# Other assumed delays and other offsets in a build-time scheduler, for two layers of segmented attention and SwiGLU

## Chip, cores and metric

One core of a Trainium2 chip runs the kernel. The metric is device time in microseconds (us) of one execution; the median of three runs before the change is 1984.57 us (1983.71 to 1984.62). In views and code the engines are called PE (TensorE, matmuls), PEld (its weight load, which overlaps the matmuls), DVE (VectorE), ACT (ScalarE), POOL (GpSimd) and SP (SyncE, which here only issues DMA transfers).

## What is computed

Two layers, each an attention part and a feed-forward part, on 2048 rows of 512 numbers, with 32 heads of 16 columns. Attention goes over four segments of 512 rows: a causal softmax inside the segment, plus a read from a running memory matrix that earlier segments filled.

```python
def _A_ref(x, wq, wk, wv, wo, beta):          # H = 32, Dh = 16, N = 4 segments of L = 512
    ...
    for s in range(N):
        qs, ks, vs = q[:, :, s], k[:, :, s], v[:, :, s]
        logits = jnp.einsum("bhqd,bhkd->bhqk", qs, ks) * scale + mask
        p = _softmax(logits, axis=-1)
        a_dot = jnp.einsum("bhqk,bhkd->bhqd", p, vs)
        pq = phi(qs)
        num = jnp.einsum("bhld,bhde->bhle", pq, M)
        den = jnp.einsum("bhld,bhd->bhl", pq, z)[..., None] + 1e-6
        outs.append(g * num / den + (1.0 - g) * a_dot)
        pk = phi(ks)
        M = M + jnp.einsum("bhld,bhle->bhde", pk, vs)
        z = z + jnp.einsum("bhld->bhd", pk)
    ...
    return o @ wo
def _B_ref(x, w_gate, w_up, w_down):          # 512 -> 1792 -> 512
    return (_silu(x @ w_gate) * (x @ w_up)) @ w_down
x = x + _A_ref(_layernorm(x), ...); x = x + _B_ref(_layernorm(x), ...)   # twice
```

## The kernel before

The program is not written in the order in which it runs. `Program.op` (L93) records 13,456 operations, each with its engine, a cost in us, a priority, and the operations that it depends on: those that wrote what it reads, that read what it overwrites, or that used its buffer before. Then `Program.issue` (L144) plays the program through once, with one clock for each engine. On the engine that can start earliest it takes, among the operations that are ready by then, the one with the lowest priority number, and emits its instruction. The result is one fixed row of instructions for each engine; on the chip every engine goes through its row in order and waits on semaphores. Two tables steer the plan. `LAT` (L38) is the delay that the planner believes lies between the end of an operation on one engine and the start of one that needs it on another. The offsets in `OFF`, `PRE` and `EP` (L30 to L32) set the priorities: in `at(v)` a number in units of one attention step (`TA`) or one feed-forward step (`TF`), from which an operation's place is worked out. Priorities do not make an operation wait; they only choose among those that are ready.

```python
            t[e] = start + o.cost
...
            end = t[e] + o.post
...
            for s in o.succ:
                s.ready = max(s.ready, end + LAT[e].get(s.eng, 0.0))
```

The work itself, in float32 that is split into a high and a low part (three matmuls in place of one, `mm3`, L281):

- **Attention** goes in 32 units a layer (4 segments, 4 head groups, 2 halves; `U`, L398). `qk_proj` (L454) projects q and k for a group (12 matmuls, L278), ScalarE copies the bank to `raw` (L464), GpSimd splits it (L465, L467), and two transfers write it to scratch memory (`scrq`, `scrk`; L479, L480), from which `load3` (L486) reads it back in another layout into `cq` and `ck` (L504, L509). `phiq` and `phik` are finished on VectorE (L474).
- `mx_units` (L514) makes the row maxima. A **score fill** (L527) writes 256, 384 or 512 columns of scores to one of two PSUM banks `pmx`, and VectorE reduces each (L534, 128 to 512 columns). The next fill of the same bank, two fills later, has to wait for those reductions. There are 768 fills in the program. The maxima are transposed (L543) and sent by a small DMA into the spare row of `cq`.
- `at_units` (L553) makes the scores again (L574, into three banks `plt`), ScalarE exponentiates them (L580), GpSimd masks the diagonal blocks (L588), and a value matmul in column groups (L603, bank `ppv`) follows.
- `mem_read` (L650) and `mem_update` (L666, L678) serve the memory; `wo_proj` projects the output; `ln_pre` and `ln_fin` make the layer norm (L349 to L361 on VectorE and GpSimd), transpose it on TensorE (L369) and copy it on ScalarE (L373) and VectorE (L374).
- **Feed-forward** (`ffn`, L800): seven chunks of 256 columns by four blocks of 512 rows; gate and up projections (L857), SiLU (L866), product (L867, L870), down projection (L884) and sum (L889). Its first steps are planned into the last attention units.

Projection matmuls (L278), and near the end of a layer those of the feed-forward part, need nothing from the engines that work on the scores. They are what the planner can put between two score matmuls: this text calls them filler. The banks `pj` are a pool of two that the planner gives out itself.

Of the kernel before, what the change touches and what calls it, by code (L numbers as in the profile page):

```python
# [26 lines left out]
WOT = ("pmx_0", "pmx_1", "pj", "pj")  # L27
EARLY_AT = (23, 25, 26)
TA, TF = 15.5, 16.7
OFF = {'qe': (0.481, 1.468), 'at': (0.2, 1.0), 'mx': (-0.666, 0.16), 'lf': (-0.709, -0.318), 'mr': (0.865, 0.781), 'mu': (0.556, 0.139), 'wo': (0.263, 1.746), 'qk': (-0.342, 0.41), 'v': (-0.3, 0.518), 'lp': (0.034, 1.108)}  # L30
PRE = {'c': -1.851, 'mb': 0.212, 'lv': -1.7, 'lo': -0.87, 'gate': -1.0, 'v': -1.534, 'dv': 0.12, 'qk1': -1.2, 'mx': -1.0}
EP = {'w': -1.935, 'wn': 0.178, 'ln': -3.0, 'dn': -0.06, 'up': -2.73}  # L32
POOL_W = ""
TABLE = 1.28
DRAIN = {("full", "cols"): 0.195, ("cols", "full"): 0.095}


LAT = dict(  # L38
    pe=dict(pe=0.01, act=0.2, dve=0.2, sp=0.19),
    act=dict(act=0.22, dve=0.13, pe=0.27, pool=0.2, sp=0.15),  # L40
    dve=dict(dve=0.13, act=0.13, pe=0.25, pool=0.16, sp=0.12),
    pool=dict(pool=0.1, dve=0.06, pe=0.13, act=0.1, sp=0.05),
    sp=dict(act=1.2, dve=1.2, pe=1.2, pool=1.2, sp=1.2),
)


# [195 lines left out]
def infini_swiglu(ctx: ExitStack, tc: tile.TileContext, x, wq, wk, wv, wo, beta, wg, wu, wd, out,  # L242
# [78 lines left out]
    def make_gate():  # L321
        for i in range(4):
            dma(lambda i=i: nc.sync.dma_start(bet.ap[32 * i:32 * i + 32],
                                              bass.AP(tensor=beta.tensor, offset=beta.offset + 2 * i,
                                                      ap=[[0, 32], [8, NG], [1, 2]])), [], [(bet, i)], kb=20)
        act(8, lambda: nc.scalar.activation(gnot.ap, bet.ap, AF.Exp), [bet], [gnot])
        dve(8, lambda: nc.vector.tensor_scalar_add(gnot.ap, gnot.ap, 1.0), [gnot], [gnot])
        dve(64, lambda: nc.vector.reciprocal(gnot.ap, gnot.ap), [gnot], [gnot])
        dma(lambda: nc.sync.dma_start(ginv.ap, bass.AP(tensor=beta.tensor, offset=beta.offset, ap=[[0, 128], [1, H]])),
            [], [ginv], kb=20)  # L330
        act(H, lambda: nc.scalar.activation(ginv.ap, ginv.ap, AF.Exp, scale=-1.0), [ginv], [ginv])
        dve(H, lambda: nc.vector.tensor_scalar_add(ginv.ap, ginv.ap, 1.0), [ginv], [ginv])
# [59 lines left out]
    def attention(lay, x_in, x_out, slots, T, hook):  # L392
# [7 lines left out]
        def at(v):  # L400
            P.prio = base + v * T

        def load_w(nm, w, tags):
            wh, wl = sb(S8[nm + "h"], T8, F32R), sb(S8[nm + "l"], T8, F32R)
            W[nm] = (wh, wl)
            for kc in range(KC):
                raw = sb(tags, [128, 512])
                dma(lambda kc=kc, raw=raw: nc.sync.dma_start(raw.ap, w[kc * 128:(kc + 1) * 128, :]), [], [raw])
                split(raw, lambda t: t, wh, wl, lambda t, kc=kc: t[:, kc, :], kc, 512)

        def load_w4(nm, w, slot):
            wh, wl = sb(S8[nm + "h"], T8, F32R), sb(S8[nm + "l"], T8, F32R)
            W[nm] = (wh, wl)
            raw = sb(S8[slot], T8)
            for kc in range(KC):
                dma(lambda kc=kc: nc.sync.dma_start(raw.ap[:, kc, :], w[kc * 128:(kc + 1) * 128, :]), [], [(raw, kc)])
                act(512, lambda kc=kc: nc.scalar.copy(wh.ap[:, kc, :], raw.ap[:, kc, :]), [(raw, kc)], [(wh, kc)],
                    sbuf=True)
                if nm in POOL_W:
                    gp(1.23, lambda kc=kc: nc.gpsimd.tensor_sub(wl.ap[:, kc, :], raw.ap[:, kc, :],  # L420
                                                                wh.ap[:, kc, :].bitcast(F32)),
                       [(raw, kc), (wh, kc)], [(wl, kc)])
                else:
                    dve(512, lambda kc=kc: nc.vector.tensor_sub(wl.ap[:, kc, :], raw.ap[:, kc, :],
                                                                wh.ap[:, kc, :].bitcast(F32)),
                        [(raw, kc), (wh, kc)], [(wl, kc)])
# [6 lines left out]
        def ln_fin(s, t, tag="pj"):  # L433
            if t == 0:
                xT[s] = (sb(S8["xh"], TX, F32R), sb(S8["xl"], TX, F32R))
            ln_transpose(XN.pop((s, t)), xT[s][0], xT[s][1], t, tag)
# [49 lines left out]
        def load3(u):  # L486
            s, n, h = U[u]
            g = GRP[s, n]
            if u < NB:
                cq = sb(S8[f"c{u}"], [128, 4, 512], F32R)  # L490
                ck = CK.get(u) or sb(f"ck{u}", [128, 2, 512], F32R)
                C3[u] = cq, ck
                pr, P.prio = P.prio, base + PRE["c"] * T
                after = [XTL] if u else []
# [147 lines left out]
        def mem_read(s, n):  # L642
            g = GRP[s, n]
            phi, m = g["phiq"], Mb[n]
            g["mem"] = mem = sb("mem", [128, 4, 128], ring=2)
            for t0 in (0, 2):
                ps, r = bank("pj"), sb("rm", [128, 2, 8, 1], ring=2)
                pv = lambda ps=ps: ps.ap[:, 0:16 * VW].rearrange("p (t h e) -> p t h e", t=2, e=VW)
                for t in range(2):
                    pe(8 * VW, 4, lambda t=t, t0=t0, ps=ps: nc.tensor.matmul(  # L650
                        ps.ap[:, 8 * VW * t:8 * VW * (t + 1)], lhsT=phi.ap[:, (t0 + t) * 128:(t0 + t + 1) * 128],
                        rhs=m.ap.rearrange("p h e -> p (h e)"), start=True, stop=True), [m, phi], [(ps, t)])
                gv = lambda: ginv.ap[:, 8 * n:8 * n + 8].rearrange("p (t h e) -> p t h e", t=1, e=1).to_broadcast([128, 2, 8, 1])
                dve(16, lambda pv=pv, r=r, gv=gv: nc.vector.scalar_tensor_tensor(
                    out=r.ap, in0=pv()[:, :, :, DH:VW], scalar=1e-6, in1=gv(), op0=OP.add, op1=OP.mult),
                    [ps, ginv], [r])
                dve(110, lambda r=r: nc.vector.reciprocal(r.ap, r.ap), [r], [r])
                dve(256, lambda pv=pv, r=r, t0=t0: nc.vector.tensor_mul(
                    mem.ap[:, t0:t0 + 2].rearrange("p t (h e) -> p t h e", e=DH), pv()[:, :, :, 0:DH],
                    r.ap.to_broadcast([128, 2, 8, DH])), [ps, r], [(mem, t0)])  # L660
# [47 lines left out]
        if lay == 0:  # L708
# [6 lines left out]
            load_w4("k", wk, "p1")  # L715
            at(PRE["lv"])
            load_w4("v", wv, "th")
            at(PRE["lo"])
            load_w4("o", wo, "tl")
# [3 lines left out]
        else:  # L723
# [5 lines left out]
            load_w("k", wk, RAW)  # L729
            at(PRE["lv"])  # L730
            load_w("v", wv, RAW)
        XTL = xT[0][0]
        at(PRE["mb"])
        for n in range(NG):
# [7 lines left out]
        if lay == 0:  # L742
            at(PRE["gate"])
            make_gate()
# [8 lines left out]
        for i, f in enumerate(mxu):  # L753
            at(PRE["mx"] + (OFF["mx"][1] - OFF["mx"][0]) * i / len(mxu))
            f()
        for u, (s, n, h) in enumerate(U):
# [3 lines left out]
            def put(units, lo, hi, rank):  # L760
                for i, f in enumerate(units):
                    items.append((u + i / max(1, len(units)) , rank, i, u + lo + (hi - lo) * (i + 0.5) / len(units), f))

            g2 = u // 2 + 2
            put(at_units(u), *OFF["at"], 0)
            if u + 1 < NU:
                put(mx_units(u + 1), *OFF["mx"], 1)
            if w8 == 4 and s + 1 < nseg:
                put([lambda t=t: ln_fin(s + 1, t) for t in range(4)], *OFF["lf"], 2)
            if h == 1 and u + 1 < NU and U[u + 1][0] > 0:  # L770
                put([lambda: mem_read(*U[u + 1][:2])], *OFF["mr"], 3)
# [28 lines left out]
    def ffn(base, x_in, x_out, slots, T):  # L800
        X, XT, Wc = {}, {}, {}

        def hold(b):
            XT[b] = (sb(slots[f"H{b}"], TX, F32R), sb(slots[f"L{b}"], TX, F32R))

        def at(v):
            P.prio = base + v * T
# [94 lines left out]
        for c in range(NF):  # L902
            for b in range(4):
                v = 4 * c + b
                if c == 0:
                    if 0 < b <= E:
                        yield
                    at(v + EP["ln"])
                    hold(b)
# [15 lines left out]
                up_at = v + (EP["up"] if v < E else 0.0)
                at(up_at)
# [68 lines left out]
```

## Time and profile before

| | us |
|---|---|
| median of three runs | 1984.57 |
| the profiled execution, first to last instruction (span) | 1980.6 |
| TensorE busy | 1929.6 |
| VectorE busy | 1139.6 |
| ScalarE busy | 759.6 |
| GpSimd busy | 473.3 |

The profile covers one execution; the 4.0 us between its span and the median are the launch and the end around it. A busy TensorE is not one at its peak: matmuls overlap, and the view sets the end of one 0.39 us after its start for 512 columns, while the next may start after 0.23 us. So an idle time of TensorE in these views begins only when the modelled end of the last matmul is past.

### The profile page before, as it was taken

How to read it: one execution, taken by the hardware profiler on the slowest of the kernel's cores; microseconds unless marked ns; L12 is line 12 of the kernel's file. 1: busy time of each engine (PE TensorE's matmuls, PEld its weight loads, DVE VectorE, ACT ScalarE, POOL GpSimd, SP SyncE). 2: the span in 40 equal slices, each digit the busy share in tenths (PEclk: the TensorE clock that was granted, in tenths of full speed). 3: DMA queues.
4: the chain of work that ended last, by engine and by line, in shares of the span. 5: the costliest groups of instructions: out<-in, count | busy, mean ns of one | idle time of the engine just before them, and what ended most of it. 6: DMA issues, size and time to landing. Idle time of an engine off the chain costs nothing. (4 is left out here: it accounts for less than half of the span.)

```text
span 1980.6 us, 31412 instructions
## 1 busy us (share of the span) xinstructions
PE 1929.6 (97%) x11136; PEld 1491.9 (75%) x11136; DVE 1139.6 (58%) x3446; ACT 759.6 (38%) x1758; POOL 473.3 (24%) x731
## 2 busy tenths in 40 slices
PE   7999999999999999999999999999999999999999
PEld 5677676776678888888876777677767788888887
DVE  6877767688644333333557677786784433333333
ACT  4655564545522212121335655555554212211211
POOL 5333443434410000000233444353343100000000
PEclk9999999999999999999999999999999999999999
DMA  7434434446131100010364353353652301100002
GB/s 245 120 111 129 129 102 146 134 155 194 54 117 33 32 22 22 22 33 22 101 192 124 105 158 123 109 151 113 181 161 70 96 11 32 32 22 11 17 1 85
DMA packets 101548, 184.00 MB, mean 93 GB/s; under 512 B 12816, under 2 KB 28176, under 8 KB 101392
## 3 DMA queue, kind: packets, MB, share of 16 engines
q1 hardware_dynamic: 99344, 181.47, 29.9%
q8 instruction: 89, 1.46, 0.3%
q10 hardware_dynamic: 2048, 0.53, 0.1%
q14 instruction: 67, 0.55, 0.1%
HBM read 114.32 MB, written 67.11 MB: 92 GB/s over the span
## 5 line engine op out<-in xcount | busy, mean ns | idle before, releaser
L857 PE MATMUL plt<-s,s 128*128 128x512 f32 x1872 | 535.6, 393 | 2.6 <-ACT s L373 2.6
L534 DVE CUSTOM_DVE_ANT_0 junk<-pmx,amask 128x128 bf16<-128x128 f32 (+3 forms) x1024 | 458.3, 482 | 98.0 <-PE pmx L527 89.3
L278 PE MATMUL pj<-s,s 128*128 128x512 f32 x1416 | 488.7, 406 | 2.8 <-DVE brs L354 1.3
L580 ACT ACTIVATE s<-plt 128x512 f32<-128x512 f32 (+2 forms) x768 | 323.5, 464 | 272.6 <-PE plt L574 153.9
L857 PEld LDWEIGHTS plt<-s,s 128*128 128x128 f32 x1872 | 351.0, 188 | 83.0 <-ACT s L373 3.8
L527 PE MATMUL pmx<-ck,s 127*128 127x256 f32 (+2 forms) x1024 | 301.4, 346 | 19.5 <-DVE mx L534 12.1
L278 PEld LDWEIGHTS pj<-s,s 128*128 128x128 f32 x1416 | 262.3, 189 | 53.4 <-issue 5.0
L574 PE MATMUL plt<-s,ck 128*128 128x256 f32 (+2 forms) x1024 | 278.5, 336 | 3.8 <-ACT s L580 2.1
L857 PE MATMUL ppv<-s,s 128*128 128x512 f32 x624 | 244.7, 393 | 0.0
L527 PEld LDWEIGHTS pmx<-ck,s 127*128 127x128 f32 x1024 | 182.5, 190 | 74.7 <-DVE mx L534 20.8
L588 POOL TENSOR_SCALAR_AFFINE_SELECT s<-s 128x512 f32<-128x512 f32 x192 | 130.4, 679 | 319.5 <-ACT s L580 311.5
L574 PEld LDWEIGHTS plt<-s,ck 128*128 128x128 f32 x1024 | 179.9, 189 | 32.8 <-ACT s L580 11.0
L884 PE MATMUL pj<-s,vt 128*128 128x512 f32 x696 | 177.5, 393 | 0.0
L884 PE MATMUL pmx<-s,vt 128*128 128x512 f32 x648 | 163.9, 394 | 0.0
L866 ACT ACTIVATE Y<-plt 128x512 f32<-128x512 f32 x52 | 31.1, 598 | 343.2 <-PE plt L857 343.2
L867 DVE TENSOR_TENSOR Y<-Y,plt 128x512 f32<-128x512 f32 x52 | 35.7, 687 | 208.9 <-ACT Y L866 207.1
L884 PEld LDWEIGHTS pj<-s,vt 128*128 128x128 f32 x696 | 130.7, 188 | 29.7 <-ACT raw L464 0.2
L884 PEld LDWEIGHTS pmx<-s,vt 128*128 128x128 f32 x648 | 121.6, 188 | 27.8 <-DVE s L889 0.2
L603 PE MATMUL ppv<-s,vt 128*32 128x512 f32 (+2 forms) x1536 | 139.2, 466 | 0.0
L857 PEld LDWEIGHTS ppv<-s,s 128*128 128x128 f32 x624 | 117.1, 188 | 26.4
L867 DVE TENSOR_TENSOR raw<-raw,ppv 128x512 f32<-128x512 f32 x52 | 35.7, 687 | 170.3 <-ACT raw L866 170.2
L351 POOL TENSOR_SCALAR bmv<-bmv 128x1 f32<-128x1 f32 x64 | 15.9, 251 | 484.2 <-DVE bmv L350 478.7
(130 smaller groups left out, 2116.2 us busy)
## 6 DMA issues: line engine op xcount, KB each, us to landing
s<-scrq SPq DMA_DIRECT2D x128, 192.0 KB, 3.3
ck<-scrk SPq DMA_DIRECT2D x128, 192.0 KB, 4.3
scrq<-s SPq DMA_DIRECT2D x32, 512.0 KB, 3.2
scrk<-s SPq DMA_DIRECT2D x32, 512.0 KB, 2.7
scrq<-s SPq DMA_DIRECT2D x32, 256.0 KB, 2.0
scrk<-s SPq DMA_DIRECT2D x32, 256.0 KB, 2.0
xin<-xmid SPq DMA_DIRECT2D x32, 256.0 KB, 2.8
s<-xmid SPq DMA_DIRECT2D x32, 256.0 KB, 3.6
```

What stands on the lines that cost most here:

```text
L278: pe(n, passes, lambda: nc.tensor.matmul(view(ps.ap), lhsT=av(a.ap), rhs=bv(b.ap), start=start, stop=stop), [(a, rk[0]), (b, rk[1])], [ps])
L351: gp(0.18, lambda: nc.gpsimd.tensor_scalar_add(mv.ap[:, 1:2], mv.ap[:, 1:2], EPS), [mv], [mv])
L527: nc.tensor.matmul(ps.ap[:, a * 256:a * 256 + nk], lhsT=cq.ap[0:127, 2 * j + p, qt * 128:(qt + 1) * 128], rhs=ck.ap[0:127, p, 0:nk], start ...
L534: dve(w, lambda a=a, qt=qt, w=w, ps=ps, junk=junk: nc.vector.tensor_tensor_reduce(out=junk.ap[:, :w], in0=ps.ap[:, a * 256:a * 256 + w], i ...
L574: nc.tensor.matmul(ps.ap[:, c0:c0 + n_], lhsT=ck.ap[:, p, k0:k0 + 128], rhs=cq.ap[:, 2 * j + p, 512 - n_:512], start=True, stop=True)
L580: act(w, lambda Pb=Pb, o0=o0, w=w, i0=i0: nc.scalar.activation(Pb.ap[:, idx, o0:o0 + w], ps.ap[:, i0:i0 + w], AF.Exp, scale=SCALE), [ps], ...
L588: gp(0.593, lambda: nc.gpsimd.affine_select(out=v(), in_=v(), pattern=[[0, 4], [1, 128]], compare_op=OP.is_ge, fill=0.0, base=0, channel_m ...
L603: nc.tensor.matmul(ps.ap[32 * i:32 * i + 32, q0:q0 + w], lhsT=vt.ap[:, kt, VW * hd:VW * hd + 32], rhs=f_[sl].ap[:, idx, c0:c0 + w], start= ...
L857: pe(512, 1, lambda i=i, j=j, kc=kc, x=x, ps=ps, wt=wt: nc.tensor.matmul(ps.ap, lhsT=wt.ap[:, i, kc, cs], rhs=XT[b][j].ap[:, :, kc], start ...
L866: act(512, lambda: nc.scalar.activation(sg.ap, pg.ap, AF.Silu), [pg], [sg], table="silu")
L867: dve(512, lambda: nc.vector.tensor_mul(sg.ap, sg.ap, pu.ap), [sg, pu], [sg])
L884: pe(512, 1, lambda i=i, j=j, fi=fi, x=x, ps=ps, wt=wt, cs=cs: nc.tensor.matmul(ps.ap, lhsT=ht.ap[:, 0:2048].rearrange("p (f a c) -> p f a ...
```

## The change

Only the tables change. In `LAT` every delay from one engine to another grows by 0.12 us, except from ScalarE to ScalarE, VectorE to VectorE, TensorE to TensorE, GpSimd to GpSimd and SyncE to SyncE. Of the offsets, some move by up to 0.8 of a step. The recorded operations, their costs, their dependencies, buffers and transfers are the same 13,456; of TensorE's 7,800 operations 7,326 stand at another place in its row, half of them by five places or fewer, none by more than 87.

```diff
-OFF = {'qe': (0.481, 1.468), 'at': (0.2, 1.0), 'mx': (-0.666, 0.16), 'lf': (-0.709, -0.318), 'mr': (0.865, 0.781), 'mu': (0.556, 0.139), 'wo': (0.263, 1.746), 'qk': (-0.342, 0.41), 'v': (-0.3, 0.518), 'lp': (0.034, 1.108)}
...
+OFF = {'qe': (1.228, 1.514), 'at': (0.2, 1.032), 'mx': (-0.666, 0.16), 'lf': (-0.412, -0.318), 'mr': (0.865, 0.751), 'mu': (0.501, 0.131), 'wo': (0.347, 1.842), 'qk': (-0.342, 0.461), 'v': (-0.3, 0.518), 'lp': (-0.001, 1.108)}
...
 LAT = dict(
-    pe=dict(pe=0.01, act=0.2, dve=0.2, sp=0.19),
-    act=dict(act=0.22, dve=0.13, pe=0.27, pool=0.2, sp=0.15),
-    dve=dict(dve=0.13, act=0.13, pe=0.25, pool=0.16, sp=0.12),
-    pool=dict(pool=0.1, dve=0.06, pe=0.13, act=0.1, sp=0.05),
-    sp=dict(act=1.2, dve=1.2, pe=1.2, pool=1.2, sp=1.2),
+    pe=dict(pe=0.01, act=0.32, dve=0.32, sp=0.31),
+    act=dict(act=0.22, dve=0.25, pe=0.39, pool=0.32, sp=0.27),
+    dve=dict(dve=0.13, act=0.25, pe=0.37, pool=0.28, sp=0.24),
+    pool=dict(pool=0.1, dve=0.18, pe=0.25, act=0.22, sp=0.17),
+    sp=dict(act=1.32, dve=1.32, pe=1.32, pool=1.32, sp=1.2),
 )
```

`PRE` and `EP` are changed in the same manner (in `PRE` the clearing of the load buffers goes from -1.851 to -1.046; in `EP` the early gate and up projections from -2.73 to -2.319).

Three places show what this does to the rows of instructions.

TensorE in the first layer, near the end of the second segment (298 us in the trace of before): score fills (`pmx`), the scores of the unit at hand (`plt`) and a memory read (`pj<-mb,phiq`). Before:

```order
L650 MATMUL pj_4025<-mb_278,phiq_3589 128x136 x2
L650 MATMUL pj_4034<-mb_278,phiq_3589 128x136 x2
L527 MATMUL pmx_4044<-ck_99,s_67 128x512
L574 MATMUL plt_4052<-s_209,ck_226 128x256 x2
L527 MATMUL pmx_4058<-ck_99,s_67 128x256 x2
L527 MATMUL pmx_4077<-ck_99,s_67 128x384
L574 MATMUL plt_4081<-s_238,ck_256 128x512
L574 MATMUL plt_4085<-s_238,ck_256 128x512
L527 MATMUL pmx_4089<-ck_99,s_67 128x512
```

The same fills after the change:

```order
L527 MATMUL pmx_4006<-ck_98,s_67 128x512
L543 MATMUL pj_4011<-ident,mx_3784 16x128
L574 MATMUL plt_4018<-s_200,ck_220 128x256 x2
L527 MATMUL pmx_4023<-ck_98,s_67 128x256 x2
L650 MATMUL pj_4032<-mb_261,phiq_3660 128x136 x2
L650 MATMUL pj_4038<-mb_261,phiq_3660 128x136
L574 MATMUL plt_4043<-s_200,ck_220 128x256 x2
L527 MATMUL pmx_4048<-ck_98,s_67 128x384
L650 MATMUL pj_4038<-mb_261,phiq_3660 128x136
L527 MATMUL pmx_4056<-ck_98,s_67 128x512
```

In both pieces the 384-column fill takes the bank that the 512-column fill has filled two fills earlier. Before, two scores matmuls and the pair of 256 stand between the two. After, there are a transpose, two more scores matmuls and three of the four memory reads as well.

TensorE in the second layer, where the last block's transposes (`pj<-ident,xn`) feed the gate and up projections of the feed-forward part (1560 us). Before:

```order
L884 MATMUL pj_17860<-s_16301,vt_17650 128x512
L369 MATMUL pj_17882<-ident,xn_17868 128x128 x4
L857 MATMUL plt_17889<-s_17754,s_15709 128x512
L857 MATMUL plt_17891<-s_17754,s_15843 128x512
L857 MATMUL plt_17889<-s_17754,s_15709 128x512
```

After:

```order
L369 MATMUL pj_17864<-ident,xn_17853 128x128 x4
L884 MATMUL pmx_17845<-s_16396,vt_17652 128x512
L884 MATMUL pj_17849<-s_16396,vt_17652 128x512
L884 MATMUL pmx_17845<-s_16396,vt_17652 128x512
L884 MATMUL pj_17849<-s_16396,vt_17652 128x512 x2
L857 MATMUL plt_17879<-s_17746,s_15661 128x512
L857 MATMUL plt_17881<-s_17746,s_15732 128x512
```

Five down projections (`L884`) have come between the transposes and the first matmul that needs their copy.

SyncE's row of transfers at the start of the first layer: the write of the first q and k to scratch, the loads of rows for the next segment's layer norm (`xin`), and the loads of `cq` (`s<-scrq`) and `ck`. Before:

```order
L480 DMA scrk_320<-s_272 128x1024
L344 DMA xin_380<-in_A_x_dram 128x512
L504 DMA s_67<-scrq_281 48x2x512 x2
L504 DMA s_209<-scrq_281 48x2x512 x2
L344 DMA xin_403<-in_A_x_dram 128x512
L509 DMA ck_99<-scrk_320 48x2x512 x2
L509 DMA ck_226<-scrk_320 48x2x512 x2
```

After:

```order
L480 DMA scrk_323<-s_280 128x1024
L504 DMA s_67<-scrq_291 48x2x512 x2
L504 DMA s_200<-scrq_291 48x2x512 x2
L344 DMA xin_393<-in_A_x_dram 128x512
L344 DMA xin_397<-in_A_x_dram 128x512
L509 DMA ck_98<-scrk_323 48x2x512 x2
L509 DMA ck_220<-scrk_323 48x2x512 x2
```

The four loads of `cq` now stand ahead of the first `xin`; both `xin` still stand ahead of the loads of `ck`.

More of the change, by code (lines that the diff above doesn't have):

```diff
@@ L29 @@
 TA, TF = 15.5, 16.7
-OFF = {'qe': (0.481, 1.468), 'at': (0.2, 1.0), 'mx': (-0.666, 0.16), 'lf': (-0.709, -0.318), 'mr': (0.865, 0.781), 'mu': (0.556, 0.139), 'wo': (0.263, 1.746), 'qk': (-0.342, 0.41), 'v': (-0.3, 0.518), 'lp': (0.034, 1.108)}
-PRE = {'c': -1.851, 'mb': 0.212, 'lv': -1.7, 'lo': -0.87, 'gate': -1.0, 'v': -1.534, 'dv': 0.12, 'qk1': -1.2, 'mx': -1.0}
-EP = {'w': -1.935, 'wn': 0.178, 'ln': -3.0, 'dn': -0.06, 'up': -2.73}
+OFF = {'qe': (1.228, 1.514), 'at': (0.2, 1.032), 'mx': (-0.666, 0.16), 'lf': (-0.412, -0.318), 'mr': (0.865, 0.751), 'mu': (0.501, 0.131), 'wo': (0.347, 1.842), 'qk': (-0.342, 0.461), 'v': (-0.3, 0.518), 'lp': (-0.001, 1.108)}
+PRE = {'c': -1.046, 'mb': 0.198, 'lv': -1.616, 'lo': -0.895, 'gate': -1.0, 'v': -1.534, 'dv': 0.337, 'qk1': -1.147, 'mx': -1.0}
+EP = {'w': -1.686, 'wn': 0.81, 'ln': -3.142, 'dn': 0.194, 'up': -2.319}
 POOL_W = ""
```

## The prediction

> **What bounds the kernel now.** First the page's busy times and its chain of work that ended last.
>
> ```profile
> span 1980.6 us, 31412 instructions
> ...
> PE 1929.6 (97%) x11136; PEld 1491.9 (75%) x11136; DVE 1139.6 (58%) x3446; ACT 759.6 (38%) x1758; POOL 473.3 (24%) x731
> ...
> PE 21%; DVE 1%; issue 0%; DVEq 0%; ACT 0%
> ```
>
> TensorE is busy 97% of the span and makes up 21 of the 22 hundredths of the chain. The matmuls stay what they are, so the change can only act on the 1980.6 - 1929.6 = 51.0 us in which TensorE idles, and on the rate at which matmuls run. Second, the busy time by stage: start, first attention, first feed-forward, second attention, second feed-forward.
>
> ```profile
> 0.00:14.00 14.00, 5.24 (x18) 3.55 (x19) 8.95 (x30) 8.43 (x13) 12.28 (x26) 1.00 0.89 299
> 14.00:560.00 546.00, 529.25 (x3657) 390.55 (x3656) 397.28 (x1440) 288.54 (x727) 220.52 (x339) 0.98 0.44 133
> 560.00:1000.00 440.00, 438.30 (x1918) 356.89 (x1917) 180.95 (x297) 94.33 (x162) 19.84 (x36) 1.00 0.14 45
> 1000.00:1560.00 560.00, 541.05 (x3748) 402.90 (x3747) 401.13 (x1452) 290.74 (x727) 220.65 (x333) 1.00 0.45 135
> 1560.00:1980.60 420.60, 415.73 (x1803) 338.05 (x1801) 151.28 (x232) 77.56 (x131) 0.00 (x0) 1.00 0.08 27
> ```
>
> Behind the window stand its length, then busy time (and instructions) of PE, PEld, DVE, ACT, POOL, then the granted clock. The feed-forward stages are full (438.30 of 440.00). The attention stages idle 546.00 - 529.25 = 16.75 and 560.00 - 541.05 = 18.95 us, together 35.7 us: this is what a better order can win, and the start's 8.8 us hangs on first loads. Third, who is waited for: microseconds in total, times, longest, for TensorE and for its weight load, whose wait begins earlier since a matmul's modelled end hides the first 0.16 us (0.39 - 0.23) of a wait from PE.
>
> ```profile
> PE pmx L527 <- DVE mx L534: 12.1, 22, 2.1
> ...
> PE plt L857 <- ACT s L373: 2.6, 4, 1.1
> PE plt L574 <- ACT s L580: 2.1, 7, 0.4
> PE pj L857 <- ACT raw L866: 1.5, 1, 1.5
> ```
>
> ```profile
> PEld pmx L527 <- DVE mx L534: 20.8, 54, 2.3
> ...
> PEld plt L574 <- ACT s L580: 11.0, 34, 0.8
> ```
>
> So most of it is score fills that wait for VectorE's reductions of the bank they take.
>
> **Score fills (L527).** One of these waits, engine by engine:
>
> ```profile
> 295.75 0.48 PE L527 MATMUL pmx<-ck,s 127*128 127x512 f32 x1
> 296.06 0.41 PE L574 MATMUL plt<-s,ck 128*128 128x256 f32 x2
> 296.30 0.40 PE L527 MATMUL pmx<-ck,s 127*128 127x256 f32 x2
> 298.78 0.44 PE L527 MATMUL pmx<-ck,s 127*128 127x384 f32 x1 [2.08 <-DVE mx L534]
> ```
>
> ```profile
> 296.43 1.68 DVE L474 SCALAR_TENSOR_TENSOR phiq<-raw,phiq 128x512 f32<-128x512 f32 x1
> 298.04 0.68 DVE L534 CUSTOM_DVE_ANT_0 junk<-pmx,amask 128x512 bf16<-128x512 f32 x1
> ```
>
> ```profile
> 296.30 1.27 POOL L467 TENSOR_TENSOR s<-raw,s 128x512 fp32r<-128x512 f32 x1
> ```
>
> The 512-column fill ends at 296.23, its reduction lasts 0.68 us, and the 384-column fill that takes the bank stands only two scores and a pair behind. I define a fill's **room**: the TensorE work between the fill whose bank it takes and itself, at the spacing of each shape, less the longest reduction of that bank. Spacing is read from starts, for 512 columns here:
>
> ```profile
> 21.80 5.04 PE L278 MATMUL plt<-s,s 128*128 128x512 f32 x21
> ```
>
> (5.04 - 0.39) / 20 = 0.23 us; a pair of 256 takes as long (296.06 to 296.30). For this fill the work between is two pairs, 0.48 us, against 0.68 of reduction and two handoffs. In the order after the change it also has a transpose, one more pair and three memory reads, together 1.17 us. Counted in both orders for all fills whose wait hangs on a reduction, 83 have under 0.3 us of room before, and 49 after; with none at all, 30 before and 14 after. The share that stays is 0.59 and 0.47; I take 0.53, nearer the waits that are long. The size of the waits lies between 12.1 us (PE) and 20.8 us (PEld); I take 18, as PE misses the start of each and all waits under 0.15 us. Of these 18 not all depend on room: at 298.78 the reduction began late because `phiq` (L474) ran 1.68 us. So I leave out 4 us, and get 14 x 0.47 = **-6.6 us** (bounds 0 and -18).
>
> **Scores (L574).** They wait for the exponentials of the bank they take. Under 0.3 us of room have 63 before and 33 after, a share of 0.52. The size is between 2.1 and 11.0 us; with 34 waits of PEld of 0.3 us in the mean I take 10, so **-4.8 us** (bounds 0 and -11).
>
> **Feed-forward boundaries.** Each of the waits of L857 for the copy of the transposes looks like this:
>
> ```profile
> 1559.64 0.63 PE L369 MATMUL pj<-ident,xn 128*128 128x128 f32 x4 [0.58 <-DVE s L889]
> 1560.94 0.73 PE L857 MATMUL plt<-s,s 128*128 128x512 f32 x2 [0.67 <-ACT s L373]
> ```
>
> ```profile
> 1560.30 0.58 ACT L373 CAST s<-pj 128x512 fp32r<-128x512 f32 x1 [4.64 <-PE pj L369]
> ```
>
> From the end of the transposes (1560.27) to the next matmul are 0.67 us, of which the copy takes 0.58. After, five matmuls stand there (5 x 0.23 = 1.15 us) and at 582 us three (0.69): 2.3 of 2.6 us go. The 1.5 us of `raw` L866 is a wait for a `pj` bank which stands among the twelve tightest of its kind before and not after. Together **-3.6 us** (bounds 0 and -4.1).
>
> **Start.** The first fill waits 2.14 us for `ck`, whose loads stood late in SyncE's row:
>
> ```profile
> 31.40 0.33 SPq L344 DMA_DIRECT2D xin<-in_A_x_dram  x1
> 31.84 1.79 SPq L504 DMA_DIRECT2D s<-scrq  x4
> 33.68 0.43 SPq L344 DMA_DIRECT2D xin<-in_A_x_dram  x1
> 34.20 1.80 SPq L509 DMA_DIRECT2D ck<-scrk  x4
> ```
>
> ```profile
> 30.61 1.53 POOL L361 TENSOR_SCALAR xn<-xin,brs 128x512 f32<-128x512 f32 x2
> ```
>
> ```profile
> 40.74 0.88 PE L527 MATMUL pmx<-ck,s 127*128 127x256 f32 x3 [2.14 <-DMA ck<-scrk]
> ```
>
> SyncE sat behind the first `xin` until L361 had freed its buffer, and the 1.79 us of issuing `cq` came on top. After, `cq` goes out before that wait; the two `xin` still hold `ck` until L361's second run ends at 32.14, so `ck` starts near 32.7 in place of 34.20: **-1.5 us** (bounds 0 and -2.1).
>
> **Clock.** Five stretches of the first layer have a granted clock below one; the first and the last two:
>
> ```profile
> 41.00:46.00 5.00, 4.49 (x18) 3.40 (x18) 4.29 (x19) 0.00 (x0) 1.83 (x3) 0.66 0.90 354
> ...
> 300.00:305.00 5.00, 5.00 (x38) 2.00 (x37) 1.85 (x7) 1.58 (x3) 0.00 (x0) 0.66 0.26 94
> 481.00:486.00 5.00, 4.63 (x36) 1.99 (x37) 1.83 (x9) 0.86 (x2) 2.89 (x5) 0.66 1.07 288
> ```
>
> A mean of 0.66 over 5 us is 3.4 us at half rate, which costs up to 1.7 us. The first and the fourth lie right behind the waits of 2.14 us (to 40.74) and 2.08 us (to 298.78). With two of the five gone: **-3.4 us** (bounds 0 and -8.5). [...]
>
> The sum: 6.6 + 4.8 + 3.6 + 1.5 + 3.4 = 19.9 us off the profiled 1980.6 gives 1960.7, and with the 4.0 us by which the median stands above the span, **1964.7 us**.
>
> **Rivals.** (A) *VectorE's stretched operations set the waits.* Margins of 0.12 us do nothing against an operation that runs a microsecond longer:
>
> ```profile
> L474 DVE SCALAR_TENSOR_TENSOR phik<-raw,phik 128x512 f32<-128x512 f32 x28 | 22.3, 796 | 3.5 <-ACT phik L472 3.5
> L474 DVE SCALAR_TENSOR_TENSOR phiq<-raw,phiq 128x512 f32<-128x512 f32 x20 | 20.1, 1003 | 4.7 <-ACT phiq L472 4.6
> ```
>
> Against the 0.68 us of a 512-column operation, L474 loses 28 x 0.12 + 20 x 0.32 = 9.8 us; at 296.43 it started behind GpSimd's L467 and ended 0.54 us after it. Both operations stay after the change, only elsewhere. Then a fifth of the first two terms is won (2.3), the boundary and the start (5.1), one clock stretch (1.7): 9.1 us, 1975.5 us. For it: the longest of all waits on VectorE is of this kind. Against: 22 and 54 waits are more than such operations explain. [...]
>
> (B) *Slower: filler runs out.* A planner that believes in longer handoffs spends projections sooner. In a layer's last segment no next segment brings new ones. Before, the second layer already shows what bare score matmuls cost:
>
> ```profile
> 1440.00:1492.00 52.00, 47.78 (x333) 33.24 (x332) 45.06 (x168) 32.45 (x82) 25.78 (x45) 1.00 0.50 143
> ```
>
> 4.22 of 52 us idle, 8%, against 18.95 of 560, 3.4%, in the layer. Were both last segments (some 230 us) like that, 230 x 0.047 = 10.8 us would come on top, and with only boundary and start won, 1984.6 + 10.8 - 5.1 = 1990.3 us. It decides from the point where more units than before have no projection between their scores. In the orders three units in a row near the end of layer two have 0, 0 and 0 projections before and 12, 0 and 14 after, in layer one 6, 0, 6 and 12, 0, 14: against it.
>
> (C) *Waits only move.* A fill placed later holds back what stood behind it, the reductions then come in bunches, and what one wait loses another gains: 1984.6 us. VectorE is busy 397.28 of 546.00 us in the first attention, so bunches take long to clear.
>
> **How the numbers follow.** Forecast 0.60 (1952 to 1972), A 0.24 (1971 to 1982), C 0.09, B 0.07. The range leaves out the slowest cases of A, C and B and the few in which nearly all of the 35.7 us go: 1948 to 1982 us. About 0.2% (4 us) is what a measurement of this kernel can tell from no change: faster, below 1980.6, holds the forecast and nearly all of A, 0.83; same takes C and A's end, 0.10; slower is B, 0.07.
>
> **What would show it.** Right: fewer than 15 waits of L527 on VectorE and under 8 us in TensorE's row; L574 under 2 us; no L857 wait on L373 at the boundaries; `ck` issued by 33 us; at most three half-rate stretches; the attention stages idle 20 to 26 us in place of 35.7, the feed-forward stages unchanged. Wrong: the same total of L527 waits with a stretched L474 in front of them (A), more idle in the last segments (B), or a feed-forward stage that is no longer full, which nothing here foresees.

## The result and the profile after

The changed kernel takes 1961.91 us (median of 4 runs, 1959.19 to 1962.29) against 1984.42 (4 runs, 1983.71 to 1984.62) before: a ratio of 0.9883, 95% interval 0.9870 to 0.9896. The forecast was 1964.7 us, its range 1948 to 1982. The profiled execution took 1962.18 us, its span is 1960.1.

The page, busy times and chain of work, as before:

```profile
span 1960.1 us, 31433 instructions
...
PE 1924.3 (98%) x11136; PEld 1492.2 (76%) x11136; DVE 1144.5 (58%) x3446; ACT 762.7 (39%) x1758; POOL 471.9 (24%) x731
...
PE 88%; DVE 5%; issue 2%; DMA 2%; ACT 2%; POOL 1%; ACTq 0%; SPq 0%; POOLq 0%; DVEq 0%
```

TensorE still bounds the kernel. Its idle time fell from 51.0 to 1960.1 - 1924.3 = 35.8 us, and its busy time by 5.3 us, together the 20.5 us between the two spans. The medians lie 22.5 us apart, because the profiled execution of before was a quick one: where a run has both numbers, its time stands 1.7 us above its span for the kernel before (48 runs) and 2.1 us for the changed one, so of the 4.0 us called launch and end at the start of this text some 2.3 are the distance of that execution from the median. The same stages as before, with PE's busy time first behind the length of the window:

```profile
14.00:560.00 546.00, 534.26 (x3714) 401.77 (x3715) 405.46 (x1454) 293.82 (x736) 221.83 (x341) 0.99 0.47 139
560.00:1000.00 440.00, 439.13 (x1900) 354.12 (x1899) 178.98 (x294) 94.78 (x160) 25.97 (x41) 1.00 0.14 45
1000.00:1560.00 560.00, 549.26 (x3803) 412.48 (x3802) 406.32 (x1450) 294.01 (x732) 211.70 (x325) 1.00 0.43 131
1560.00:1960.10 400.10, 396.34 (x1705) 320.11 (x1704) 145.01 (x220) 71.52 (x119) 0.00 (x0) 1.00 0.08 26
```

The windows are fixed times, so what was won shows in two ways: less idle (11.74 and 10.74 us in the attention stages, 22.5 in place of 35.7), and more matmuls inside the same window (3714 where 3657 were, 3803 where 3748 were). Who is waited for, first in TensorE's row, then in that of its weight load:

```profile
PE pmx L527 <- DVE mx L534: 8.8, 20, 1.6
PE plt L369 <- ACT xn L358: 7.3, 2, 6.8
PE pj L650 <- DVE s L374: 2.7, 2, 1.4
...
PE plt L574 <- DMA s<-nm: 1.6, 4, 0.8
...
PE pmx L527 <- DMA ck<-scrk: 1.1, 2, 0.9
...
PE plt L574 <- ACT s L580: 0.3, 1, 0.3
```

```profile
PEld pmx L527 <- DVE mx L534: 14.0, 43, 1.1
...
PEld plt L574 <- ACT s L580: 6.7, 23, 0.7
```

Before, the fills had 12.1 us (22) and 20.8 (54), the scores 2.1 (7) and 11.0 (34). The two waits of L857, 4.1 us together, are gone from the list.

### The profile page after: what moved, and what is told of

Read it like the earlier page. It is cut to its first block, busy times and chain, and to the rows that moved or that the text cites. A ratio compares the mean times of both kernels' runs of the same rounds, so it can differ in the third digit from the quotient of the medians.

```text
span 1960.1 us, 31433 instructions
## 1 busy us (share of the span) xinstructions
PE 1924.3 (98%) x11136; PEld 1492.2 (76%) x11136; DVE 1144.5 (58%) x3446; ACT 762.7 (39%) x1758; POOL 471.9 (24%) x731
## 4 chain that ended last, share of the span: by engine, by line
PE 88%; DVE 5%; issue 2%; DMA 2%; ACT 2%; POOL 1%; ACTq 0%; SPq 0%; POOLq 0%; DVEq 0%
PE plt L857 22%; PE pj L278 15%; PE pj L884 8%; PE pmx L527 8%; PE pmx L884 8%; PE ppv L857 7%; PE plt L574 7%; PE ppv L603 7%; DVE junk L534 2%; PE pj L857 2%; PE pj L369 1%; PE pmx L278 1%; PE pj L650 1%; DMA scrk<-s 1%; DMA s<-nm 1%
## 5 line engine op out<-in xcount | busy, mean ns | idle before, releaser
L857 PE MATMUL plt<-s,s 128*128 128x512 f32 x1872 | 540.8, 395 | 0.0
L278 PE MATMUL pj<-s,s 128*128 128x512 f32 x1416 | 494.2, 406 | 1.1 <-DVE s L889 0.3
L857 PEld LDWEIGHTS plt<-s,s 128*128 128x128 f32 x1872 | 351.6, 188 | 83.4 <-ACT s L373 0.4
L527 PE MATMUL pmx<-ck,s 127*128 127x256 f32 (+2 forms) x1024 | 301.4, 344 | 11.7 <-DVE mx L534 8.8
L574 PE MATMUL plt<-s,ck 128*128 128x256 f32 (+2 forms) x1024 | 279.7, 334 | 2.3 <-DMA s<-nm 1.6
L884 PE MATMUL pj<-s,vt 128*128 128x512 f32 x696 | 257.2, 395 | 0.0
L857 PE MATMUL ppv<-s,s 128*128 128x512 f32 x624 | 245.9, 395 | 0.0
L884 PE MATMUL pmx<-s,vt 128*128 128x512 f32 x648 | 243.7, 395 | 0.0
L527 PEld LDWEIGHTS pmx<-ck,s 127*128 127x128 f32 x1024 | 184.3, 190 | 63.5 <-DVE mx L534 14.0
L574 PEld LDWEIGHTS plt<-s,ck 128*128 128x128 f32 x1024 | 181.7, 189 | 29.6 <-ACT s L580 6.7
L867 DVE TENSOR_TENSOR Y<-Y,plt 128x512 f32<-128x512 f32 x52 | 35.8, 688 | 224.8 <-PE plt L857 215.1
L884 PEld LDWEIGHTS pj<-s,vt 128*128 128x128 f32 x696 | 130.5, 188 | 31.1 <-PE pmx L884 0.6
L884 PEld LDWEIGHTS pmx<-s,vt 128*128 128x128 f32 x648 | 121.6, 188 | 27.9
L857 PEld LDWEIGHTS ppv<-s,s 128*128 128x128 f32 x624 | 117.1, 188 | 27.5
L867 DVE TENSOR_TENSOR raw<-raw,ppv 128x512 f32<-128x512 f32 x52 | 35.7, 687 | 143.9 <-PE ppv L857 136.4
```

Source lines behind the costliest of these rows:

```text
L278: pe(n, passes, lambda: nc.tensor.matmul(view(ps.ap), lhsT=av(a.ap), rhs=bv(b.ap), start=start, stop=stop), [(a, rk[0]), (b, rk[1])], [ps])
L527: nc.tensor.matmul(ps.ap[:, a * 256:a * 256 + nk], lhsT=cq.ap[0:127, 2 * j + p, qt * 128:(qt + 1) * 128], rhs=ck.ap[0:127, p, 0:nk], start ...
L574: nc.tensor.matmul(ps.ap[:, c0:c0 + n_], lhsT=ck.ap[:, p, k0:k0 + 128], rhs=cq.ap[:, 2 * j + p, 512 - n_:512], start=True, stop=True)
L857: pe(512, 1, lambda i=i, j=j, kc=kc, x=x, ps=ps, wt=wt: nc.tensor.matmul(ps.ap, lhsT=wt.ap[:, i, kc, cs], rhs=XT[b][j].ap[:, :, kc], start ...
L867: dve(512, lambda: nc.vector.tensor_mul(sg.ap, sg.ap, pu.ap), [sg, pu], [sg])
L884: pe(512, 1, lambda i=i, j=j, fi=fi, x=x, ps=ps, wt=wt, cs=cs: nc.tensor.matmul(ps.ap, lhsT=ht.ap[:, 0:2048].rearrange("p (f a c) -> p f a ...
```

## Experiments

All kernels were timed in three rounds beside the kernel before, whose median was 1984 to 1986 us in them. Several expectations speak of **missing room**. It extends the prediction's room from fills to every operation of TensorE that waits for another engine: how far its room (TensorE's work in between, at the spacings of before's trace, less the operation waited for) falls short of 0.6 us, summed over the program. It is counted in the planned rows before a kernel runs. The table gathers what follows; "tight fills" is the same sum for L527 alone and short of 0.3 us, which was worked out only once all had run. Fill and `nm` waits are microseconds in TensorE's row of the one profiled execution.

| kernel | median us | ratio, 95% interval | missing room | tight fills | fill waits | nm waits |
|---|---|---|---|---|---|---|
| before | 1984.42 | 1 | 140.7 | 21.6 | 12.1 | 0.8 |
| after | 1961.91 | 0.9883 [0.9870, 0.9896] | 67.1 | 11.8 | 8.8 | 1.6 |
| delays_only | 1981.17 | 0.9981 [0.9970, 0.9991] | 112.3 | 24.2 | 11.1 | 3.4 |
| offsets_only | 1988.38 | 1.0012 [1.0003, 1.0022] | 134.3 | 25.6 | 12.3 | 1.5 |
| undo_off | 1973.85 | 0.9939 [0.9925, 0.9954] | 113.3 | 23.5 | 11.3 | 0.8 |
| undo_pre | 1972.75 | 0.9933 [0.9918, 0.9947] | 92.5 | 19.6 | 10.1 | 4.8 |
| undo_ep | 1965.69 | 0.9902 [0.9885, 0.9918] | 74.0 | 13.3 | 10.1 | 2.1 |
| off_and_delays | 1963.74 | 0.9902 [0.9881, 0.9923] | 73.0 | 13.5 | 10.1 | 1.7 |
| loop_delays | 1978.50 | 0.9977 [0.9967, 0.9988] | 79.1 | 20.9 | 15.3 | 4.8 |
| delays_double | 1992.15 | 1.0032 [1.0019, 1.0045] | 97.2 | 24.3 | 10.1 | 12.3 |
| transfer_longer | 1983.17 | 0.9996 [0.9985, 1.0006] | 98.6 | 20.8 | 15.5 | 2.0 |

### Delays alone, offsets alone

delays_only is the kernel before with the new `LAT`; offsets_only is the changed kernel with the old one.

```diff
 # delays_only, against before
-    pe=dict(pe=0.01, act=0.2, dve=0.2, sp=0.19),
+    pe=dict(pe=0.01, act=0.32, dve=0.32, sp=0.31),
...
 # offsets_only, against before
-OFF = {'qe': (0.481, 1.468), 'at': (0.2, 1.0), ...
+OFF = {'qe': (1.228, 1.514), 'at': (0.2, 1.032), ...
```

> The new delays with the old offsets. Counted in its order, 95 score fills stand with under 0.3 us of room (83 before the change, 49 after it), 42 scores matmuls (63, 33), 8 feed-forward matmuls behind their transposes (13, 1). Theory 1, the longer delays alone make the room: 1960 to 1968 us, L527 waits on VectorE at 9 us or less in TensorE's row. Theory 2, room in the order sets the time, and it came from delays and offsets together: the fills win nothing, scores and boundaries about 5 us, 1976 to 1984 us, L527 on VectorE at 11 to 14 us.

> The old delays with the new offsets. Counted in its order: 88 tight fills, 45 tight scores, 7 tight feed-forward matmuls. Theory 1, the delays alone: no change, 1982 to 1988 us. Theory 2, room, from both together: 1976 to 1984 us with L527 on VectorE at 11 to 14 us. Theory 3, the new places alone carry it: 1960 to 1968 us.

The delays alone bring 0.2%, the offsets alone cost 0.1%; together they bring 1.2%. The 1981.17 us and the 11.1 us of fill waits of delays_only are what its Theory 2 gave; 1988.38 us of offsets_only lies just above all three of its ranges. Neither table has more than a small gain of its own to add to the other's. An offset names a place in the order that the planner makes with its delays; another set of delays makes another order, and the same offsets then put fills at other distances. Waits in the weight load's row of offsets_only:

```profile
PEld pmx L527 <- DVE mx L534: 26.1, 73, 1.7
...
PEld plt L574 <- ACT s L580: 11.9, 41, 0.8
```

73 fill waits, more than the 54 of before.

### Without GpSimd's second operand (rival A)

L467 makes the low part of q and k on GpSimd from two operands. Here it writes zeros, so the low parts of q and k are left out of what the kernel computes; the number of operations stays, in before and in after.

```diff
-            gp(1.23, lambda: nc.gpsimd.tensor_sub(nat.ap[:, a, 1, :], raw.ap, nat.ap[:, a, 0, :].bitcast(F32)),
+            gp(1.23, lambda: nc.gpsimd.memset(nat.ap[:, a, 1, :].bitcast(F32), 0.0),
```

> The kernel before, in the same order, with GpSimd's subtraction that makes the low part of q and k (L467, 1.31 us) replaced by a clearing that reads nothing; the low part of q and k is left out of the result. It tells what VectorE's stretched operations cost on TensorE's path. If they set the waits (rival A): L474 falls to 0.7 us and the time by 8 to 12 us, to 1973 to 1977 us. If they are the 4 us that the prediction left out: 1978 to 1982 us. If they lie beside other work: within 2 us of 1984.4.

> The same replacement in the changed kernel, its order unchanged; the low part of q and k is left out. If rival A's waits were all left over by the change: 8 to 12 us off, 1950 to 1954 us. If 4 us: 1956 to 1960 us. If the new order hides them: within 2 us of 1961.9.

1972.49 us (ratio 0.9930, 0.9913 to 0.9946) from before, and 1953.91 (0.9836, 0.9821 to 0.9850) from after. So the stretched operations, with all that hangs on them, are worth some 13 us in before (1985.4 - 1972.5 = 12.9), and 1961.9 - 1953.9 = 8.0 in after: the 8 to 12 us of rival A, or more, and not the 4 us that the prediction left out. By the ratios it is 13.9 and 9.3 us, each with over 3 us either way, so that after loses less is likely and not certain. L474 in no_split_before, by lines:

```profile
L474 DVE SCALAR_TENSOR_TENSOR phik<-raw,phik 128x512 f32<-128x512 f32 x28 | 20.9, 745 | 3.3 <-ACT phik L472 3.2
L474 DVE SCALAR_TENSOR_TENSOR phiq<-raw,phiq 128x512 f32<-128x512 f32 x20 | 14.4, 718 | 4.7 <-ACT phiq L472 4.6
```

and in after:

```profile
L474 DVE SCALAR_TENSOR_TENSOR phik<-raw,phik 128x512 f32<-128x512 f32 x28 | 26.6, 950 | 8.6 <-ACT phik L472 8.3
L474 DVE SCALAR_TENSOR_TENSOR phiq<-raw,phiq 128x512 f32<-128x512 f32 x20 | 19.3, 967 | 1.3 <-ACT phiq L472 1.3
```

With zeros written, the same instruction takes 0.72 to 0.75 us; in after it is as stretched as in before (0.95 and 0.97, against 0.80 and 1.00). The change did not remove the stretching. What part of the fill waits hangs on it, the weight load's rows say, in no_split_before and no_split_after:

```profile
PEld pmx L527 <- DVE mx L534: 16.3, 49, 1.4
```

```profile
PEld pmx L527 <- DVE mx L534: 7.7, 24, 1.0
```

Before has 20.8 us of them, so 4.5 go with the subtraction; after has 14.0, so 6.3 go. These waits the change did not reduce; what it reduced are the others, from 16.3 to 7.7. In no_split_after TensorE's waits for the transfer of the row maxima rose to 7.5 us, where after has 1.6, so the 8.0 us are what is left when that is paid. The zeros also take GpSimd 0.53 us where the subtraction takes 1.31, so a part of the 13 and 8 us may be the split that is ready sooner; the runs don't part the two. How the subtraction lengthens L474, no run shows.

### Each table of offsets put back

Three kernels are the changed one with `OFF`, `PRE` or `EP` as before (the diff of the change, one line reversed).

> The changed kernel with the table OFF of before (delays, PRE and EP stay new). Room theory, with its measure: the room that is missing to 0.6 us, summed over all of TensorE's operations, is 140.7 us before the change and 67.1 us after it, for 22.5 us of time, so 0.31 us of time for 1 us; here it is 113.3 us, so 1976 us. Tight fills 95. If the delays or the other two tables carry the gain: 1960 to 1966 us.

> The changed kernel with the table PRE of before. Room theory: 92.5 us of missing room (69 tight fills), so 1970 us. If PRE, which only places the start of each layer, acts on the start alone: 1962 to 1965 us.

> The changed kernel with the table EP of before. Room theory: 74.0 us of missing room (51 tight fills, 4 tight feed-forward matmuls in place of 1), so 1964 us, with 1 to 2 us of waits of L857 back at the boundaries. If EP is worth the whole boundary term of the prediction: 1965.5 us.

1973.85, 1972.75 and 1965.69 us: to put `OFF` or `PRE` back costs 11.9 and 10.8 us, `EP` 3.8, and the missing room has the three times within 3 us. As shares of the whole they would sum to 26.5 us, where only 19.3 lie between delays_only and after; with some 3 us either way on each, that alone does not settle it. One more kernel asks for this: new delays and `OFF`, old `PRE` and `EP`.

> The kernel before with the new delays and the new OFF; PRE and EP are the old ones. Theory (the room in front of each TensorE operation decides): missing room 73.0 us, against 140.7 before and 67.1 after, so some 1964 us (1961 to 1968). Rival (what the three tables bring adds up): undo_pre cost 10.9 us and undo_ep 3.8 us against the changed kernel, so without both 1961.9 + 14.7 = 1976.6 us (1973 to 1980).

1963.74 us, as the room says and 13 us below the sum of the single losses (10 us by the ratios, more than their intervals allow). With the new `EP`, the old `PRE` costs 10.8 us; with the old `EP` (undo_ep, 1965.69, the same ratio of 0.9902), nothing. Two numbers of the plan that lie in different tables decide together where an operation stands. With this run the change is down to two parts that need each other, `LAT` and `OFF`, and they hold all but 2 us of the gain (4 us by the ratios).

### The delays doubled

The changed kernel with 0.24 us in place of 0.12 on the same delays.

```diff
-    pe=dict(pe=0.01, act=0.32, dve=0.32, sp=0.31),
+    pe=dict(pe=0.01, act=0.44, dve=0.44, sp=0.43),
...
```

> The changed kernel with delays that are 0.24 us longer than before in place of 0.12. If a longer assumed delay by itself makes the row safer: 1955 to 1962 us; the median room of fills does grow, from 0.96 to 1.06 us. Room theory: the tight end decides, and there 48 fills have under 0.15 us (28 after the change, 45 before it), 97.2 us of missing room, so 1971 us.

1992.15 us, slower than before by 0.3%: the expectation by room fails by 21 us. The waits of TensorE in this kernel:

```profile
PE plt L574 <- DMA s<-nm: 12.3, 9, 3.2
PE pmx L527 <- DVE mx L534: 10.1, 25, 1.6
...
PE plt L574 <- ACT s L580: 2.8, 9, 0.5
```

On top stands a wait that before had 0.8 us of: the scores need the row maxima, which go by a transpose (L543), a copy (L545) and a small transfer of their own (L546, `nm`). The longest one, on TensorE:

```profile
64.12 0.27 PE L543 MATMUL pj<-ident,mx 128*16 128x128 f32 x1
...
67.97 0.68 PE L527 MATMUL pmx<-ck,s 127*128 127x384 f32 x2
71.88 0.97 PE L574 MATMUL plt<-s,ck 128*128 128x512 f32 x3 [3.23 <-DMA s<-nm]
```

and ScalarE with its queue:

```profile
65.32 0.25 ACT L545 ACTIVATE nm<-pj 16x128 fp32r<-16x128 f32 x1
...
65.60 0.53 ACTq L546 DMA_DIRECT2D s<-nm  x1
```

The transfer is issued 1.2 us behind the end of the transpose, and the scores start at 71.88, over 6 us later; TensorE runs out of other work at 68.65. The missing room did not see this, since it counts one handoff and not a chain of three engines and a transfer. To the planner this transfer lands 2.2 us after its issue, a number of its own that did not grow with the delays (the delay from ScalarE to TensorE comes on top). Of the 64 transfers, 24 had under 3.5 us of TensorE work between transpose and scores in delays_double, against 9 in after. The next kernel changes only that number.

```diff
-                    nm.ap.bitcast(F32)), [nm], [(cq, "m")]).post = 2.2
+                    nm.ap.bitcast(F32)), [nm], [(cq, "m")]).post = 3.0
```

> delays_double with one number more changed: the planner takes the transfer of the row maxima (L546, nm) as landing 3.0 us after its issue in place of 2.2. Theory: delays_double lost its time to the 12.3 us in which the scores (L574) wait for that transfer, since the longer delays push the maxima late and the 2.2 us did not grow with them. Of the 64 transfers 24 had under 3.5 us of TensorE work between the transpose of the maxima and the first scores; now 7 have. Then the wait of L574 for nm falls under 5 us and the time to 1975 to 1984 us. Rival (doubled delays spend the filler too early, or the room at fills alone decides): the missing room stays as it was (97.2 and 98.6 us), so by the rival the time stays at 1988 to 1995 us, whatever becomes of that wait.

1983.17 us, 9.0 below delays_double, and the wait is down:

```profile
PE pmx L527 <- DVE mx L534: 15.5, 36, 1.6
...
PE plt L574 <- DMA s<-nm: 2.0, 2, 1.8
```

The transfers themselves, by the view of their line, are no faster. In delays_double and in transfer_longer:

```profile
DMA to landing us min/median/max: 1.8/2.3/6.8
```

```profile
DMA to landing us min/median/max: 1.8/2.3/6.0
```

So 10.3 us of this wait went between the two profiles, and 9.0 us of the median (7 by the ratios to before). The profiles exaggerate: that of delays_double is its slowest run of nine (1997.5 us), that of transfer_longer one of its fast ones (1981.5). The time lies in the range that the theory gave and outside the rival's: without this wait the doubled delays are no longer slower than before. What is left between transfer_longer and after, 21 us, is elsewhere: the fill waits rose to 15.5, and that is the order itself.

### Which delays

The changed kernel with 0.12 us only between TensorE and VectorE and between TensorE and ScalarE.

```diff
-    dve=dict(dve=0.13, act=0.25, pe=0.37, pool=0.28, sp=0.24),
+    dve=dict(dve=0.13, act=0.13, pe=0.37, pool=0.16, sp=0.12),
...
```

> The changed kernel, with the 0.12 us only on the delays between TensorE and VectorE and between TensorE and ScalarE, in both directions; all other delays are the old ones. Theory (room): missing room 79.1 us, so some 1966 us (1963 to 1970), as it is those two loops that the fills and the scores wait in. Rival (the offsets fit only the order planned with all of the new delays): most of the gain goes, 1975 to 1986 us; and the maxima's transfer has under 3.5 us of TensorE work ahead of its scores in 14 units, against 9 in the changed kernel, so that L574 waits for nm over 4 us.

1978.50 us: four fifths of the gain are gone (a ratio of 0.9977 where after has 0.9883), though the missing room is only 79.1. The rival's range holds. The waits:

```profile
PE pmx L527 <- DVE mx L534: 15.3, 38, 1.0
...
PE plt L574 <- DMA s<-nm: 4.8, 6, 1.7
```

The `nm` wait is the 4 us that the rival named. But the larger part are fills, 15.3 us where after has 8.8, and those the missing room should have seen. It did in its fills' share (52.9 us of the 79.1, against 34.2 in after), but counted against them scores with more room than in after (18.3 and 24.4 us), and those could bring little, as the scores wait 0.3 us in TensorE's row of after and 6.7 in the weight load's. The missing room is no sure guide: of the nine kernels from which its 0.31 us was not taken, it has four within about 3 us (the three with one table put back, and off_and_delays) and sets five too fast, by 5 us (delays_only), 6 (offsets_only), 12 (transfer_longer), 13 (loop_delays) and 21 (delays_double). Over the eleven kernels of the table, the time goes with the missing room at a correlation of 0.71 and with the tight fills at 0.89. That second figure was found with the results at hand, no run has tried it, and it ranks undo_off (23.5, 1973.9 us) beside delays_only (24.2, 1981.2); what parts these two stays open.

## Why the prediction held, step by step

- **Score fills (-6.6).** The weight load's waits fell from 20.8 to 14.0, by 6.8 us; TensorE's own from 12.1 to 8.8. By the weight load's row the size is right, by TensorE's own it is half. Without the subtraction the waits fall from 16.3 to 7.7, a share of 0.47 that stays, where the step took 0.53, and the 4.5 us that go with it in before are near the 4 us left out: here the mechanism holds too. The mark set for it (fewer than 15 waits, under 8 us) was missed: 20 waits and 8.8 us. The piece of the order shown from 298 us lost its wait of 2.08 us. TensorE in after, where the same fills are now:

```profile
285.64 0.47 PE L527 MATMUL pmx<-ck,s 127*128 127x512 f32 x1
...
288.27 0.34 PE L527 MATMUL pmx<-ck,s 127*128 127x384 f32 x1
288.45 0.40 PE L650 MATMUL pj<-mb,phiq 128*128 128x136 f32 x2
288.59 0.48 PE L527 MATMUL pmx<-ck,s 127*128 127x512 f32 x1
```

From the start of the 512-column fill to that of the 384-column one that takes its bank are now 2.63 us of work, and there is no bracket behind it. But room is not all that changed here. VectorE in after:

```profile
287.10 0.68 DVE L534 CUSTOM_DVE_ANT_0 junk<-pmx,amask 128x512 bf16<-128x512 f32 x1
...
289.09 0.68 DVE L474 SCALAR_TENSOR_TENSOR phiq<-raw,phiq 128x512 f32<-128x512 f32 x1
```

`phiq` (L474), which before ran 1.68 us in front of this reduction, now comes behind it. Before, the reduction ended 298.72 - 295.75 = 2.97 us after its fill's start, so behind such an L474 the 2.63 us of work would still have left some 0.3 us of wait (an estimate). The order of VectorE's row gave a part of what this piece won.

- **Scores (-4.8).** From 11.0 to 6.7 in the weight load's row, 4.3 us; 0.3 us are left in TensorE's own. Right. The maxima's transfer gave 0.8 of it back (0.8 to 1.6), so that L574 waits 2.3 us in all.
- **Feed-forward boundaries (-3.6).** The chain between transposes and the gate and up projections, in after:

```profile
1534.73 0.60 PE L369 MATMUL pj<-ident,xn 128*128 128x128 f32 x4
1535.09 0.48 PE L884 MATMUL pmx<-s,vt 128*128 128x512 f32 x1
1535.40 0.40 PE L884 MATMUL pj<-s,vt 128*128 128x512 f32 x1
1535.64 0.39 PE L884 MATMUL pmx<-s,vt 128*128 128x512 f32 x1
1535.87 0.63 PE L884 MATMUL pj<-s,vt 128*128 128x512 f32 x2
1536.34 5.97 PE L857 MATMUL plt<-s,s 128*128 128x512 f32 x25
```

The five down projections stand where the copy was waited for, and no bracket is left. Right, though the two parts of the step, 2.3 and 1.5, add up to 3.8 and not 3.6; the 4.1 us are gone from these waits. About 1.8 came back at another user of the `pj` banks: the memory read L650 waits 2.7 us for L374, where it waited 0.9 before. Of the four boundary waits two lay at 582 and 1560.94 us, inside the feed-forward windows; with these 1.3 us those stages idle 0.9 and 3.8 us where they idled 1.7 and 4.9, and not "unchanged".

- **Start (-1.5).** The loads of `ck` went out earlier, as said and further: at 31.66 in place of 34.20. The time was not won. SyncE and TensorE in after:

```profile
30.45 1.11 SPq L344 DMA_DIRECT2D xin<-in_A_x_dram  x2
31.66 1.79 SPq L509 DMA_DIRECT2D ck<-scrk  x4
```

```profile
37.83 0.57 PE L527 MATMUL pmx<-ck,s 127*128 127x256 f32 x3
39.97 0.90 PE L527 MATMUL pmx<-ck,s 127*128 127x512 f32 x3 [1.56 <-DVE mx L534]
```

The first fills run at 37.83 rather than 40.74, and then the third waits 1.56 us for a reduction. VectorE's row says why:

```profile
38.25 0.16 DVE L354 SCALAR_TENSOR_TENSOR brs<-bmv,brs 128x1 f32<-128x1 f32 x1 [0.64 <-POOL brs L352]
39.11 0.16 DVE L354 SCALAR_TENSOR_TENSOR brs<-bmv,brs 128x1 f32<-128x1 f32 x1 [0.70 <-POOL brs L352]
39.18 0.28 DVE L534 CUSTOM_DVE_ANT_0 junk<-pmx,amask 128x128 bf16<-128x128 f32 x1
```

The reductions stood behind two steps of the layer norm that themselves waited for GpSimd. The step that failed is that an earlier `ck` is time won: the wait of 2.14 us went, and what was next in line was VectorE's row. TensorE's idle time in the first 60 us fell by 0.6 us (47.63 busy before, 48.27 after).

- **Clock (-3.4).** The profiled execution has four windows of 3.4 us at half rate (granted clock 0.50 inside them, as in before; at 14, two from 41, at 471 us) in place of five, so in it one was won and not two, and the mark of at most three was missed. The longest stretch, two windows:

```profile
41.00:47.80 6.80, 6.16 (x17) 4.97 (x17) 3.71 (x17) 0.00 (x0) 1.96 (x2) 0.51 0.90 252
```

The two waits on which the step rested are gone, but that such a wait brings a window is not shown. In after the windows from 41 and at 471 us stand behind waits of 1.56 and 1.36 us; undo_ep has the same two waits, 1.37 us at 467.31 and the one shown here, and no window behind either (granted clock 1.0 over that execution, to three places):

```profile
39.27 0.89 PE L527 MATMUL pmx<-ck,s 127*128 127x512 f32 x3 [1.54 <-DVE mx L534]
```

```profile
36.00:50.00 14.00, 11.13 (x48) 7.71 (x47) 11.59 (x50) 2.70 (x5) 7.75 (x12) 1.00 0.82 261
```

Over runs the size holds better: the mean granted clock was 0.9954 before (48 runs) and 0.9975 after (4). Within a kernel the time falls by 1.44 us for each 0.001 of granted clock (75 runs of the experiments and of after, each against its kernel's mean, correlation -0.78), so 0.0021 are 3.0 us. One such window lowers the mean by 3.4 x 0.5 / 1980 = 0.00086 and so costs 1.24 us by that slope (an estimate), where the step took 1.7. The clock does not follow the waits from kernel to kernel either: delays_only, whose fills wait almost as long as before's, has a mean of 0.9985 against 0.9952 in the runs of before beside it. By the same slope that is 4.8 us, as much as the 4.2 us that it won.

- **The sum.** Waits as the two traces have them, fills and scores in the weight load's row, the others in TensorE's: fills 6.8 us less, scores 4.3, boundaries 4.1, `ck` 3.4 (4.5 to 1.1 in all; its later waits stood in no term), against 1.8 more at L650 and 0.8 at the maxima's transfer: 16.0 us, and one half-rate window, 1.2. That is 17.2 of the 20.5 us between the spans. The other 3.3 us are not assigned. That 1964.7 came within 3 us of 1961.9 is in part luck: in these executions the start gave 0.6 us of its 1.5 and the clock 1.2 of its 3.4, and what is not assigned stands in for them.
- **Rivals.** C (waits only move) falls with 22.5 us of idle in place of 35.7. B (filler runs out) falls in this change; a like case, slower than before by longer delays, came with delays_double, but by the maxima's transfer and not by missing projections. A is half right: its time of 1975.5 is missed by 14 us, though its cause is real. It was given 4 us of the fills' term, and of the fill waits 4.5 us do go with the subtraction; but the time that goes with it is some 13 us in before and 8 in after. The half-rate windows were a term of their own there, and part of them may belong to A: without the subtraction one such window is left in the profile of before and none in after's (granted clock 0.999 and 1.0), where there were five and four, 5 us in each pair at 1.24 us a window. Over all runs it is less: the mean granted clock went from 0.9954 to 0.9972 and from 0.9975 to 0.9985, which by the slope is 2.6 us of the 13 and 1.4 of the 8. What the rest is made of, stretching or an earlier split, the runs don't part.

## What to carry to other kernels

In a planned order look at the tight end of the distances: how many of the operations that wait for another engine have almost no work in front, not how much there is in the mean. Where a plan has assumed delays and hand-fitted places, change and try them together, and go through every number by which the planner knows a time: one that stays behind (here the landing of a small transfer) becomes the next wait. And when a wait goes at the head of a row, read the row of the engine that feeds the next instruction before booking the gain.

## What the runs showed of the hardware that was not expected

The half-rate windows of the TensorE clock (0.50 for 3.4 us) stand mostly behind waits of TensorE of 1.3 to 2.1 us, but not behind each such wait. Of the nine in the profiles of before and after, seven follow one of these, the two from 41 us in after the same one; the one at 471 us in after follows the wait of 1.36 us at 469.55 shown below. Two, at 51 and 481 us in before, follow shorter waits (0.35 us at 49.90 and 0.73 at 481.37). And no_split_after has waits of 1.55, 2.02, 1.36 and 1.64 us (at 39.56, 142.72, 464.74 and 1433.28) without a single window (granted clock 1.0). What decides stays open. The granted clock differs from one execution to the next of the same kernel (0.996 to 0.999 in the four runs of after, times 1959.19 to 1962.29), as three or four windows more or fewer would make it, and by the slope above each costs about 1.2 us (both estimates).

```profile
469.55 0.73 PE L650 MATMUL pj<-mb,phik 128*128 128x136 f32 x4 [1.36 <-DVE s L374]
```

The small transfer of the row maxima lands after 1.8 us at best and in the median of before and after, with single ones up to 6.4 and 5.4 us; in delays_double the median is 2.3 and the longest 6.8 us. There, the 2.2 us that the plan takes for it are too few for at least half of the 64.
